# Fused attention and GELU kernel: batch 0's loads issued at once, weights in quarters, scores transposed by DMA

## The chip, the cores and the metric

The kernel runs on one core of one Trainium2 chip. Times are device microseconds of a whole execution; profiles give a span from the first to the last instruction, some 2 us shorter. PE is TensorE, PEld its weight loads, DVE is VectorE, ACT is ScalarE, POOL is GpSimd, and SP is the engine that issues most DMAs here.

## The reference

Four batches of cross-covariance attention (256 x 256 scores, summed over 6080 rows) feed a two-layer network with a tanh GELU.

```python
q, k, v = three arrays of (4, 6080, 256), float32          # tau = 1.0
qn = q / (norm(q, axis=1) + 1e-06);  kn = likewise k
s  = kn.transpose(0, 2, 1) @ qn / tau                      # (4, 256, 256)
a  = softmax(s, axis=-1)
x  = (v @ a).reshape(24320, 256)
y  = gelu_tanh(x @ w_in) @ w_out                           # w_in 256 x 2048, w_out 2048 x 256
```

## The kernel before

The product `a @ w_in` is formed first (`aw`), so each block of 512 rows needs only `hp = aw.T @ vT` (2048 x 512), the GELU on ACT into `g`, and `yp = g.T @ w_out`. Batch 0's q and k must be loaded, multiplied (`G`) and normalised before anything else can start. The same work for batches 1 to 3 is spread in small steps between the matmuls of the batch before: eight steps per block, twelve blocks per batch. Below, a slot is 128 rows, a chunk is the slots that one pair of loads (q and k) brings, and the column sums are the sums of squares from which the norms come. Of the loop over chunks (cut):

```python
first_chunks = chunks_of([12, 12, 5, 6, 4, 4, 2, 2], 2)   # slots of 128 rows of batch 0
fillers = [0, 0, 5, 7, 4, 3, 1, 0]                        # dummy matmuls meant to keep PE's clock up
...
for n, ch in enumerate(first_chunks):
    for to, sq, x in todo:
        nc.vector.tensor_copy(to, x)                       # fp32 -> bf16, DVE
        nc.scalar.activation(sq, x, AF.Square)             # ACT
    keep_clock(fillers[n])
    for s, rows in slots_of(ch, 128):
        gram(G, qkb, s, rows, ...)                         # 2 matmuls a slot
    pairs_of(n, sqb)          # pair sums on DVE, then column sums on PE (some chunks: sums only)
    ...                       # issue the loads of later chunks into the buffers now free
```

In the steps of a later batch (cut):

```python
for n in range(16):                       # the first 16 steps
    if n in (3, 9): load_qk(b, n // 6)    # loads of q and k of batch b, cast to bf16 by the DMA
    if b == 1 and n == 5: turn_v_on_pe(1) # block 1's v: 8 transposes on PE
    yield
...                                       # 54 steps: G and squares, then the norms
T = turned(Gs)                            # 4 fp32 transposes on PE
...
rsinv = row_sums(eT)
for fs in range(4):
    for ic in range(2):
        aw_part(eT, rsinv, aw_next, fs, ic); yield
```

From block 2 on, v is transposed by DMA two blocks ahead: `turn_v(nb + 2)` issues four DMA transposes of 128 x 256 on SP, `load_v(nb + 3)` loads v on POOL's queue.

## Time and profile before

The median of the runs was 754.13 us. These are the landmarks, from the timeline of the trace, in us from the start of the span:

| landmark | us |
|---|---|
| last piece of batch 0's q and k lands | 34.28 |
| last column sum of batch 0 starts on PE | 35.78 |
| first `hp` matmul starts | 40.06 |
| last `hp` matmul starts | 740.28 |
| end of the span | 751.98 |

I use two intervals of it as measures: **the start of the first `hp`**, which tells what the loading part costs, and **the time from the first to the last `hp`** (700.22 us), which tells what the stream costs. Both are read from one trace of each kernel.

### The profile page before, as it was taken

The page shows a single profiled execution, that of the slowest core. Times are in us where ns is not written, and L with a number is a line of the kernel's source. Part 1 is how long each engine was busy: PE and PEld are TensorE (multiplying, and loading weights), DVE is VectorE, ACT ScalarE, POOL GpSimd, SP SyncE. Part 2 cuts the span into 40 slices and gives each one's busy share as a digit, 9 for nine tenths or more (in the row PEclk, how much of TensorE's full clock was granted, in tenths as well). Part 3 has the DMA queues.
Part 4 walks back from the last instruction along what each step waited for, and adds up shares of the span by engine and source line. Part 5 has one row for each costly group of instructions (what it writes and reads, how often), then busy time and mean ns, then how long its engine had stood idle before and what let it go on. Part 6 is the DMA issues. An engine that isn't in the chain of part 4 may idle for free.

```text
span 752.0 us, 12341 instructions
## 1 busy us (share of the span) xinstructions
PE 726.4 (97%) x5186; PEld 502.3 (67%) x5274; DVE 284.3 (38%) x497; ACT 420.3 (56%) x411; POOL 80.8 (11%) x154
## 2 busy tenths in 40 slices
PE   2899999999999999999999999999999999999998
PEld 1656766776666766776666666776666666666666
DVE  3733556463501646554521265555351011011011
ACT  4875555556456555555555555555645655555552
POOL 1061111101012102101001102010101000000000
PEclk9999999999999999999999999999999999999999
DMA  9989685613237685824325876671413533322111
GB/s 369 400 205 200 104 150 139 132 43 69 70 72 144 114 163 108 164 63 75 71 57 117 141 119 124 150 143 46 69 43 85 105 85 70 69 75 54 41 57 57
DMA packets 80183, 85.69 MB, mean 114 GB/s; under 512 B 55424, under 2 KB 59136, under 8 KB 79616
## 3 DMA queue, kind: packets, MB, share of 16 engines
q0 software_dynamic: 14480, 30.87, 25.7%
q1 hardware_dynamic: 65344, 52.39, 24.4%
q10 hardware_dynamic: 304, 1.64, 0.5%
q8 instruction: 41, 0.67, 0.4%
q14 instruction: 14, 0.11, 0.0%
HBM read 78.91 MB, written 24.90 MB: 138 GB/s over the span
## 4 chain that ended last, share of the span: by engine, by line
PE 94%; DMA 3%; ACT 1%; issue 1%; DVE 0%; POOL 0%; SPq 0%; DVEq 0%; POOLq 0%
PE yp L528 44%; PE hp L602 43%; PE G L158 4%; PE ps L218 2%; ACT sq L269 1%; DMA st<-in_q_dram 1%; DMA st<-in_k_dram 1%; PE T L196 0%; POOL wout_bf L359 0%; PE yp L633 0%; PE cols L170 0%; DVE qk L267 0%; DVE aw L413 0%; DVE Gs L188 0%; ACT eT L383 0%
## 5 line engine op out<-in xcount | busy, mean ns | idle before, releaser
L606 ACT ACTIVATE g<-hp 128x1024 bf16<-128x1024 f32 (+1 forms) x384 | 389.8, 1015 | 307.0 <-PE hp L602 295.2
L528 PE MATMUL yp<-wout_bf,g 128*128 128x256 bf16 x3024 | 392.0, 273 | 1.6 <-POOL wout_bf L359 0.7
L602 PE MATMUL hp<-vT,aw 128*128 128x512 bf16 (+1 forms) x1456 | 383.9, 377 | 3.8 <-DVE aw L413 0.2
L528 PEld LDWEIGHTS <-g 128*128 128x128 bf16 x3024 | 295.9, 98 | 114.3 <-issue 1.2
L602 PEld LDWEIGHTS <-aw 128*128 128x128 bf16 x1536 | 149.9, 98 | 104.1 <-DVE aw L413 0.5
L545 DVE COPY ysb<-yp 128x512 f32<-128x512 f32 (+1 forms) x95 | 64.9, 683 | 396.5 <-PE yp L528 396.5
L460 DVE TENSOR_TENSOR acc<-acc,sq 128x512 f32<-128x512 f32 x141 | 97.6, 692 | 4.8
L459 DVE TENSOR_TENSOR sq<-qkb 128x512 bf16<-128x512 bf16 x141 | 58.9, 418 | 0.0
L158 PE MATMUL G<-qkb 128*128 128x256 bf16 x288 | 55.0, 273 | 0.0
L307 POOL DMA_DIRECT2D vb<-in_v_dram x47 | 25.9, 552 | 88.6 <-DMA vT<-vb 81.3
L227 DVE TENSOR_SCALAR aw<-ps,rsinv 128x512 bf16<-128x512 f32 x30 | 22.4, 749 | 23.5 <-PE ps L218 18.3
L158 PEld LDWEIGHTS <-qkb 128*128 128x128 bf16 x288 | 28.2, 98 | 3.3
L332 POOL CAST gate<-g 1x1 f32<-1x1 bf16 x24 | 5.9, 245 | 227.8 <-ACT g L606 227.8
L158 PE MATMUL G<-qk 128*128 128x256 bf16 x96 | 13.5, 298 | 15.8 <-DVE qk L267 15.8
L269 ACT ACTIVATE sq<-st 128x3072 bf16<-128x3072 f32 (+2 forms) x9 | 21.1, 2379 | 11.1 <-DMA st<-in_q_dram 8.2
L158 PEld LDWEIGHTS <-qk 128*128 128x128 bf16 x96 | 9.8, 106 | 19.1 <-DVE qk L267 16.6
L267 DVE CAST qk<-st 128x3072 bf16<-128x3072 f32 (+2 forms) x10 | 14.2, 1438 | 13.1 <-DMA st<-in_q_dram 10.0
L218 PE MATMUL ps<-win_bf,eT 128*128 128x512 bf16 x54 | 16.4, 379 | 0.2
L479 POOL TENSOR_TENSOR r<-r,half 128x4 f32<-128x4 f32 x3 | 3.1, 1042 | 103.4 <-DVE r L478 103.4
L82 POOL DMA_DIRECT2D qkb<-in_q_dram x24 | 12.9, 537 | 5.8 <-issue 4.3
L585 POOL COPY g<-gr 128x1024 bf16<-128x1024 bf16 x2 | 2.1, 1036 | 101.3 <-PE yp L528 101.3
L82 POOL DMA_DIRECT2D qkb<-in_k_dram x24 | 12.9, 539 | 0.0
(73 smaller groups left out, 109.0 us busy)
## 6 DMA issues: line engine op xcount, KB each, us to landing
out_dram<-ysb SPq DMA_DIRECT2D x44, 512.0 KB, 3.0
vb<-in_v_dram POOLq DMA_DIRECT2D x43, 256.0 KB, 6.2
qkb<-in_q_dram POOLq DMA_DIRECT2D x21, 384.0 KB, 4.6
qkb<-in_k_dram POOLq DMA_DIRECT2D x21, 384.0 KB, 6.4
st<-in_q_dram SPq DMA_DIRECT2D x2, 1536.0 KB, 11.8
vT<-vb SPq DMA_TRANSPOSE x184, 3.0
wst<-in_moe_w_in_dram SPq DMA_DIRECT2D x4, 512.0 KB, 7.5
wst<-in_moe_w_out_dram SPq DMA_DIRECT2D x2, 1024.0 KB, 11.7
```

Source lines behind the costliest of these rows:

```text
L82: engines[x].dma_start(out=dst[x][:, 0:size, :], in_=src[b, s0 * 128 : (s0 + size) * 128, :].rearrange("(p s) c -> p s c", s=size))
L158: nc.tensor.matmul(G[:, ic, :], lhsT=qk[1][:rows, s, ic * 128 : ic * 128 + 128], rhs=qk[0][:rows, s, :], start=first and ic == 0, stop=las ...
L218: nc.tensor.matmul(ps, lhsT=eT[:, jc, ic * 128 : ic * 128 + 128], rhs=win_bf[:, jc, fs * 512 : fs * 512 + 512], start=jc == 0, stop=jc == 1)
L227: nc.vector.tensor_scalar_mul(dst, ps, scale)
L269: nc.scalar.activation(sq, x, AF.Square)
L307: nc.gpsimd.dma_start(out=t[:, 0:n, :], in_=v_rows[r0 : r0 + n * 128, :].rearrange("(p s) c -> p s c", s=n))
L459: nc.vector.tensor_mul(sq[:rows], flat, flat)
L460: nc.vector.tensor_add(acc[:rows], acc[:rows], sq[:rows])
L528: nc.tensor.matmul(yp[:rows, at, :], lhsT=g[:, fc, s * 128 : s * 128 + rows], rhs=wout_bf[:, fc, :], start=fc == 0, stop=fc == FC - 1)
L545: nc.vector.tensor_copy(ysb[:, s0 : s + 1, :], yp[:, 0 : s + 1 - s0, :])
L602: nc.tensor.matmul(hp[:, j, :cols], lhsT=aw[:, cc, fc * 128 : fc * 128 + 128], rhs=vT[:, cc, :cols], start=cc == 0, stop=cc == 1)
L606: nc.scalar.activation(g[:, 2 * i : 2 * i + 2, :cols], hp[:, :, :cols], AF.Gelu_apprx_tanh)
```

## The change

Its intent: (1) batch 0's loads get homes of their own (the still unused tiles of `g`, `aw` and the staging pool), so that no load waits for a buffer; (2) the weights come in quarters, with output-weight rows contiguous per partition, for which the columns of `aw` are sorted; (3) the scores of batches 1 to 3 leave PE: their fp32 bits are split into upper and lower halves, turned by DMA and put together again, and the row sums come two steps later; (4) the chain to the first `hp` is cut finer. The core of the diff, with cuts marked:

```diff
-    first_chunks = chunks_of([12, 12, 5, 6, 4, 4, 2, 2], 2)
-    fillers = [0, 0, 5, 7, 4, 3, 1, 0]
+    first_chunks = chunks_of([2, 12, 12, 5, 4, 4, 4, 2, 1, 1], 3)
+    fillers = [0, 0, 0, 5, 6, 5, 4, 2, 1, 0]
+    CASTS_POOL = (6, 7)
...
+    g_homes = [gp.tile([128, FC, 512], BF16, tag="g", name="g").bitcast(FP32) for _ in range(2)]
+    aw_homes = [...]; st_homes = [...]
+    for n, ch in enumerate(first_chunks):
+        load_chunk((nc.sync, nc.scalar if n < 1 else nc.sync), staged[n][0], 0, ch, 2)
...
-        for x in ((2, 3) if n == 0 else (4, 5) if n == 1 else (n + 4,)):
-            stage_chunk(x)
...
+    for fs in range(4):
+        w, T = w_quarter(), t_of(fs)
+        rows_of_w = moe_w_out[fs * 512 : fs * 512 + 512, :]
+        nc.sync.dma_start(out=w.rearrange("p (e t c) -> p e t c", t=T, c=256),
+                          in_=rows_of_w.rearrange("(e p t) c -> p e t c", p=128, t=T))
+        nc.gpsimd.tensor_copy(wout_bf[:, fs * 4 : fs * 4 + 4, :], w.rearrange(...))
...
-        T = turned(Gs)
+        bits = Gs.bitcast(U16).rearrange("p a (j h) -> p h a j", h=2)
+        for h in range(2):
+            nc.vector.tensor_copy(apart[:, h], bits[:, h])
+            for ic in range(2):
+                nc.sync.dma_start_transpose(
+                    out=crossed[:, h, :, ic * 128 : ic * 128 + 128], in_=apart[:, h, ic, :])
+        for _ in range(6):
+            yield
+        bits = T.bitcast(U16).rearrange("p a (i h) -> p h a i", h=2)
+        for h in range(2):
+            nc.vector.tensor_copy(bits[:, h], crossed[:, h])
```

More of the change, by code (lines that the diff above doesn't have):

```diff
@@ L10 @@
 BF16 = mybir.dt.bfloat16
+U16 = mybir.dt.uint16
 AF = mybir.ActivationFunctionType
@@ L93 @@
     n_all = S_ALL + 1
-    first_chunks = chunks_of([12, 12, 5, 6, 4, 4, 2, 2], 2)
-    TAIL, SHARED = 4, 6
-    fillers = [0, 0, 5, 7, 4, 3, 1, 0]
-    staged = []
+    first_chunks = chunks_of([2, 12, 12, 5, 4, 4, 4, 2, 1, 1], 3)
+    n_chunks = len(first_chunks)
+    TAIL = 4
+    fillers = [0, 0, 0, 5, 6, 5, 4, 2, 1, 0]
+    SQUARES_DVE = (6, 7)
+    CASTS_POOL = (6, 7)
     def halves(pool, tag, dtype, size, most=SMAX):
@@ L107, in halves, with slot_pair @@
         return [t.rearrange("p a b c -> p (a b) c") for t in tiles], None
-    def stage_chunk(n):
-        if n < len(first_chunks):
-            _, size, rem = first_chunks[n]
-            if n < SHARED:
-                st, whole = halves(stage, "st", FP32, size)
-            else:
-                _, size, rem = first_chunks[n - 2]
-                whole = staged[n - 2][1][:, :, size + rem :, :]
-                st = [whole[:, x] for x in range(2)]
-                rem = False
-            if rem:
-                nc.gpsimd.memset(whole[:, :, size, :], 0.0)
-            load_chunk((nc.sync, nc.scalar if n < 1 else nc.sync), st, 0, first_chunks[n], 2)
-            staged.append((st, whole))
-    for n in range(2):
-        stage_chunk(n)
+    def slot_pair(whole, lo, hi):
+        return [whole[:, x, lo:hi, :] for x in range(2)], whole[:, :, lo:hi, :]
+    g_homes = [gp.tile([128, FC, 512], BF16, tag="g", name="g").bitcast(FP32) for _ in range(2)]
+    aw_homes = [awp.tile([128, 2, D], BF16, tag="aw", name="aw").bitcast(FP32).rearrange(
+        "p x (s c) -> p x s c", c=256) for _ in range(2)]
+    st_homes = [stage.tile([128, 2, SMAX, 256], FP32, tag="st", name="st") for _ in range(4)]
+    shared = st_homes[3]
+    staged = [
+        slot_pair(shared, 0, 2),
+        ([g[:, 0:12, :] for g in g_homes], None),
+        ([t.rearrange("p a b c -> p (a b) c") for t in st_homes[:2]], None),
+        slot_pair(st_homes[2], 0, 6),
+        slot_pair(aw_homes[0], 0, 4),
+        slot_pair(aw_homes[1], 0, 4),
+        ([g[:, 12:16, :] for g in g_homes], None),
+        slot_pair(shared, 2, 4),
+        slot_pair(shared, 4, 5),
+        slot_pair(shared, 5, 6),
+    ]
+    nc.gpsimd.memset(staged[3][1][:, :, 5, :], 0.0)
+    for n, ch in enumerate(first_chunks):
+        load_chunk((nc.sync, nc.scalar if n < 1 else nc.sync), staged[n][0], 0, ch, 2)
     ident = const.tile([128, 128], FP32)
@@ L147, with t_of, sorted_columns, pieces @@
     win_v = moe_w_in.rearrange("(c p) d -> p c d", p=128)
-    wout_v = moe_w_out.rearrange("(t p) d -> p t d", p=128)
+    def t_of(fs):
+        return 2 if fs == 0 else 4
+    def sorted_columns(ps, fs):
+        return ps.rearrange("a (e p t) -> a e t p", p=128, t=t_of(fs))
+    def pieces(dst, fs):
+        return dst.rearrange("a (e t p) -> a e t p", p=128, t=t_of(fs))
     def keep_clock(n, pool=pH, tag="h"):
@@ L190, in scaled, with row_sums @@
         return Gs
-    def turned(Gs):
-        T = pA.tile([128, 2, 256], FP32, tag="a", name="T")
-        for ic in range(2):
-            for jc in range(2):
-                nc.tensor.matmul(T[:, jc, ic * 128 : ic * 128 + 128],
-                                 lhsT=Gs[:, ic, jc * 128 : jc * 128 + 128],
-                                 rhs=ident, is_transpose=True)
-        return T
-    def row_sums(eT):
-        rs = pA.tile([128, 512], FP32, tag="a", name="rs")
+    def row_sums(eT, rs=None):
+        if rs is None:
+            rs = pA.tile([128, 512], FP32, tag="a", name="rs")
         for ic in range(2):
@@ L212, in row_sums, with aw_part @@
         return rsinv
-    def aw_part(eT, rsinv, aw, fs, ic, ps=None, act=False):
+    def aw_part(eT, rsinv, aw, fs, ic, ps=None):
         if ps is None:
@@ L222, in aw_part @@
                 start=jc == 0, stop=jc == 1)
-        dst, scale = aw[:, ic, fs * 512 : fs * 512 + 512], rsinv[:, ic : ic + 1]
-        if act:
-            nc.scalar.activation(dst, ps, AF.Copy, scale=scale)
-        else:
-            nc.vector.tensor_scalar_mul(dst, ps, scale)
+        dst = pieces(aw[:, ic, fs * 512 : fs * 512 + 512], fs)
+        nc.vector.tensor_scalar_mul(dst, sorted_columns(ps, fs), rsinv[:, ic : ic + 1])
     G = pA.tile([128, 2, 256], FP32, tag="a", name="G")
     cols = pA.tile([128, 512], FP32, tag="a", name="cols")
-    n_chunks = len(first_chunks)
     seen, summed = 0, 0
@@ L265 @@
             todo = [[y[:, :, 0:hi] for y in (qk_whole, sq_whole, whole)]]
+        if n in CASTS_POOL:
+            nc.gpsimd.tensor_copy(qkb[1][:, 0:hi], st[1])
+            todo = [(qkb[0][:, 0:hi], None, st[0])]
         for to, sq, x in todo:
-            nc.vector.tensor_copy(to, x)
-            if n != n_chunks - 2:
-                nc.scalar.activation(sq, x, AF.Square)
-        if n == n_chunks - 2:
-            nc.scalar.activation(sqb[1][:, 0:hi], st[1][:, 0:hi], AF.Square)
+            nc.vector.tensor_copy(to[:, 0:hi] if whole is None else to, x)
+            if sq is not None and n not in SQUARES_DVE:
+                nc.scalar.activation(sq[:, 0:hi] if whole is None else sq, x, AF.Square)
+        if n in SQUARES_DVE:
+            nc.scalar.activation(sqb[1][:, 0:hi], st[1], AF.Square)
             nc.vector.tensor_mul(sqb[0][:, 0:hi], qkb[0][:, 0:hi], qkb[0][:, 0:hi])
@@ L279 @@
             waiting = None
-        if n < 2:
+        if n < 3:
             pairs_of(n, sqb)
@@ L343, in load_qk, with w_quarter @@
             loaded_of[b, n] = views, t
-    def flat_stage(n):
-        w = stage.tile([128, 2, SMAX, 256], FP32, tag="st", name="wst")
-        return w.rearrange("p a b c -> p (a b c)")[:, 0:2048].rearrange("p (c d) -> p c d", c=n)
-    for half in range(2):
-        w = flat_stage(2)
-        for x in range(2):
-            c0 = half * 1024 + x * 512
-            nc.sync.dma_start(out=w[:, :, x * 512 : x * 512 + 512], in_=win_v[:, :, c0 : c0 + 512])
-            nc.gpsimd.tensor_copy(win_bf[:, :, c0 : c0 + 512], w[:, :, x * 512 : x * 512 + 512])
-        load_v(1 + half)
-    for half in range(2):
-        w = flat_stage(8)
-        nc.sync.dma_start(out=w, in_=wout_v[:, half * 8 : half * 8 + 8, :])
-        nc.gpsimd.tensor_copy(wout_bf[:, half * 8 : half * 8 + 8, :], w)
+    w_homes = []
+    def w_quarter():
+        n = len(w_homes)
+        if n % 3 == 0:
+            t = stage.tile([128, 2, SMAX, 256], FP32, tag="st", name="wst")
+            t = t.rearrange("p a b c -> p (a b c)")
+        else:
+            t = w_homes[-1]
+        w_homes.append(t)
+        return t[:, n % 3 * 1024 : n % 3 * 1024 + 1024]
+    for fs in range(4):
+        w = w_quarter().rearrange("p (c d) -> p c d", c=2)
+        step = 256 if fs == 0 else 512
+        for lo in range(0, 512, step):
+            c0 = fs * 512 + lo
+            nc.sync.dma_start(out=w[:, :, lo : lo + step], in_=win_v[:, :, c0 : c0 + step])
+            nc.gpsimd.tensor_copy(win_bf[:, :, c0 : c0 + step], w[:, :, lo : lo + step])
+        if fs % 2:
+            load_v(1 + fs // 2)
+    for fs in range(4):
[3 more added lines that the diff above has]
+                          in_=rows_of_w.rearrange("(e p t) c -> p e t c", p=128, t=T))
+        nc.gpsimd.tensor_copy(wout_bf[:, fs * 4 : fs * 4 + 4, :], w.rearrange("p (f c) -> p f c", c=256))
     r = smx.tile([128, 4], FP32, tag="r", name="r")
@@ L366, with turn_v0 @@
     Gs = scaled(G, r)
-    vps = []
-    for cc in range(2):
-        p = pH.tile([128, 2, 512], FP32, tag="h", name="vps")[:, 0, :]
+    vps = pH.tile([128, 2, 512], FP32, tag="h", name="vps")
+    spare = pH.tile([128, 2, 512], FP32, tag="h", name="spare")
+    def turn_v0(cc):
         for s in range(4):
-            nc.tensor.matmul(p[:, s * 128 : s * 128 + 128],
+            nc.tensor.matmul(vps[:, cc, s * 128 : s * 128 + 128],
                              lhsT=v0[:, s, cc * 128 : cc * 128 + 128],
                              rhs=ident, is_transpose=True)
-        vps.append(p)
-    keep_clock(1, pY, "y")
-    T = turned(Gs)
-    keep_clock(1, pY, "y")
+    turn_v0(0)
+    T = [pY.tile([128, 512], FP32, tag="y", name="T") for _ in range(2)]
+    for ic in range(2):
+        for jc in range(2):
+            nc.tensor.matmul(T[jc][:, ic * 128 : ic * 128 + 128],
+                             lhsT=Gs[:, ic, jc * 128 : jc * 128 + 128],
+                             rhs=ident, is_transpose=True)
+    turn_v0(1)
     vT0 = vts.tile([128, 2, 512], BF16, tag="vT", name="vT")
-    nc.vector.tensor_copy(vT0[:, 0, :], vps[0])
+    nc.vector.tensor_copy(vT0[:, 0, :], vps[:, 0, :])
     eT = smx.tile([128, 2, 256], BF16, tag="eT", name="eT")
@@ L382, with first_aw @@
     for jc in range(2):
-        nc.scalar.activation(eT[:, jc, :], T[:, jc, :], AF.Exp, scale=r[:, jc : jc + 1])
-    nc.scalar.activation(vT0[:, 1, :], vps[1], AF.Copy)
+        nc.scalar.activation(eT[:, jc, :], T[jc][:, 0:256], AF.Exp, scale=r[:, jc : jc + 1])
+    nc.scalar.activation(vT0[:, 1, :], vps[:, 1, :], AF.Copy)
     firsts = []
-    def first_aw(n, jc, pool=pY, tag="y"):
+    def first_aw(n, jc, pool=pA, tag="a"):
         if jc == 0:
@@ L400 @@
     first_aw(1, 0)
-    rsinv = row_sums(eT)
+    rsinv = row_sums(eT, spare[:, 0, :])
     first_aw(0, 1)
@@ L404 @@
     for n in (2, 3):
-        first_aw(n, 0, pA, "a")
+        first_aw(n, 0, pY, "y")
         first_aw(n, 1)
-    for n in range(4):
+    for n, t, act in ((0, 0, False), (1, 0, True), (0, 1, True), (1, 1, False), (2, None, False), (3, None, False)):
         ic, lo = n % 2, n // 2 * 256
-        dst, scale = aw[:, ic, lo : lo + 256], rsinv[:, ic : ic + 1]
-        if n == 1:
-            nc.scalar.activation(dst, firsts[n][:, 0:256], AF.Copy, scale=scale)
+        dst = aw[:, ic, lo : lo + 256].rearrange("a (t p) -> a t p", t=2)
+        ps = firsts[n][:, 0:256].rearrange("a (p t) -> a t p", t=2)
+        if t is not None:
+            dst, ps = dst[:, t], ps[:, t]
+        scale = rsinv[:, ic : ic + 1]
+        if act:
+            nc.scalar.activation(dst, ps, AF.Copy, scale=scale)
         else:
-            nc.vector.tensor_scalar_mul(dst, firsts[n][:, 0:256], scale)
+            nc.vector.tensor_scalar_mul(dst, ps, scale)
     nc.scalar.activation(dummy, ones_f, AF.Gelu_apprx_tanh)
-    aw_left = [(fs, ic, *((pA, "a") if fs == 2 else (pY, "y"))) for fs in range(1, 4) for ic in range(2)]
+    aw_left = [(fs, ic, *((pY, "y") if fs == 2 else (pA, "a"))) for fs in range(1, 4) for ic in range(2)]
     def more_aw(n):
@@ L486, in attention_steps @@
         Gs = scaled(G, r)
+        apart = split.tile([128, 2, 2, 256], U16, tag="apart", name="apart")
+        crossed = split.tile([128, 2, 2, 256], U16, tag="crossed", name="crossed")
+        T = split.tile([128, 2, 256], FP32, tag="T", name="T")
+        bits = Gs.bitcast(U16).rearrange("p a (j h) -> p h a j", h=2)
+        for h in range(2):
+            nc.vector.tensor_copy(apart[:, h], bits[:, h])
+            for ic in range(2):
+                nc.sync.dma_start_transpose(
[5 more added lines that the diff above has]
+            nc.vector.tensor_copy(bits[:, h], crossed[:, h])
         yield
-        yield
-        T = turned(Gs)
         eT = smx.tile([128, 2, 256], BF16, tag="eT", name="eT")
@@ L495, in attention_steps @@
         else:
-            th = smx.tile([128, 2, 256], FP32, tag="th", name="th")
-            den = smx.tile([128, 2, 256], FP32, tag="den", name="den")
+            th = split.tile([128, 2, 256], FP32, tag="th", name="th")
+            den = split.tile([128, 2, 256], FP32, tag="den", name="den")
             for jc in range(2):
@@ L507, in attention_steps @@
                     op0=ALU.add, op1=ALU.mult)
+            yield
+            yield
             yield
```

## The prediction

Passages that no trace of this case shows are cut from it (and from two expectations below), and the cuts are marked. The sum has all its terms, -1.3 - 0.7 - 0.3 + 0 = -2.3 us. In the hand count of the loading part the terms are cut: 23 dummies, 44 `G` matmuls at 0.109 us and 80 column sums at 0.025 us came to 11.7 us with a figure for a dummy that the trace doesn't show; at the 0.216 us between two dummies in the trace they come to 11.8.

> **What bounds the kernel now.** I read the page first (totals, slices, chain), then a table of stretches, then what the TensorE (PE) waited for, then the timeline of the first 52 us and of one place in mid-run. From the page:
>
> ```profile
> PE 726.4 (97%) x5186; PEld 502.3 (67%) x5274; DVE 284.3 (38%) x497; ACT 420.3 (56%) x411; POOL 80.8 (11%) x154
> ...
> L528 PE MATMUL yp<-wout_bf,g 128*128 128x256 bf16 x3024 | 392.0, 273 | 1.6 <-POOL wout_bf L359 0.7
> L602 PE MATMUL hp<-vT,aw 128*128 128x512 bf16 (+1 forms) x1456 | 383.9, 377 | 3.8 <-DVE aw L413 0.2
> ```
>
> PE has hardly any idle time, and its two large groups wait 5.4 us in all. The list of PE's waits is as short:
>
> ```profile
> PE G L158 <- DVE qk L267: 15.8, 3, 14.4
> PE yp L528 <- POOL wout_bf L359: 0.7, 1, 0.7
> ```
>
> So only the first 40 us and one wait of 0.7 us are open to better scheduling. The table of stretches (columns: length, busy time of PE, weight loads, DVE, ACT, POOL, granted clock, DMA share, GB/s) says what the first 40 us are:
>
> ```profile
> 10.00:20.00 10.00, 5.08 (x48) 3.82 (x48) 7.95 (x6) 9.10 (x4) 1.07 (x1) 1.00 1.00 420
> 20.00:35.00 15.00, 14.06 (x176) 10.65 (x178) 11.68 (x14) 12.11 (x7) 0.00 (x0) 1.00 1.03 402
> 35.00:40.00 5.00, 4.10 (x46) 2.90 (x44) 2.57 (x9) 3.91 (x9) 2.70 (x3) 1.00 1.04 340
> ```
>
> From 10 to 35 us the DMA engines are full (share 1.00 and more) at 402 to 420 GB/s while batch 0's q and k come in. After that a short serial chain (roots, scaling, transposes, exponential, first products) leads to the first `hp` matmul at 40.06 us, and from there PE runs to 748 us practically without a hole. Is PE at its true rate there? The timeline at 182 us answers (start, length, then the instructions merged):
>
> ```profile
> 182.42 1.04 PE L528 MATMUL yp<-wout_bf,g 128*128 128x256 bf16 x8
> 182.62 1.02 ACT L606 ACTIVATE g<-hp 128x1024 bf16<-128x1024 f32 x1 [0.71 <-PE hp L602]
> 183.19 0.47 PEld L196 LDWEIGHTS T<-ident,Gs 128*128 128x128 f32 x4
> 183.30 0.60 PE L196 MATMUL T<-ident,Gs 128*128 128x128 f32 x4
> ```
>
> Eight `yp` matmuls in 1.04 us, the last one 0.273 long, start (1.04 - 0.273) / 7 = 0.11 us apart; likewise the four fp32 transposes `T`, (0.60 - 0.273) / 3 = 0.109. They stand flush between their neighbours. Each matmul taken out of this stream is worth its spacing, not its 0.273 us.
>
> [...]Here a DMA transpose takes 3.0 us from issue to landing (median)[...].
>
> **The change part by part.**
>
> *Scores turned by DMA (batches 1 to 3).* Removed from PE: 4 transposes x 3 batches x 0.109 = **1.3 us**, all on the path. Added: per batch 4 DMA transposes, and 4 DVE copies of 128x512 16-bit elements with a step of two, which I put at the 0.69 us of this page's 128x512 DVE rows[...]: 3 x 4 x 0.69 = 8 us of DVE, idle for 62% of the span. The copies back come six steps later. A step (4 `hp` at 0.216 and 8 `yp` at 0.109) is 1.74 us, so the transposes have about 10 us: issue takes 1.3 us each on SP, landing 3. That fits. Count of steps: 81 before the last products, now 88, plus 8, is 96, exactly the 12 blocks x 8 steps of a batch. The last products fall in the last steps, but those hold the columns that the next batch uses last, six steps on. No wait follows.
>
> *Row sums two steps later.* Before, neither they nor the products after them made PE wait in mid-run (they aren't in the list of waits). **0 us.**
>
> *Weights in quarters, output weights in contiguous rows.* The timeline at 50 us shows the one wait there is:
>
> ```profile
> 49.88 1.90 POOL L359 CAST wout_bf<-wst 128x2048 bf16<-128x2048 f32 x1 [2.02 <-PE hp L602]
> ...
> 51.83 0.60 PE L528 MATMUL yp<-wout_bf,g 128*128 128x256 bf16 x4 [0.71 <-POOL wout_bf L359]
> ```
>
> The second 1 MB half of the output weights landed at 49.8 us and took a 1.9 us cast. [...]casts of about 1.0 us per quarter, bring the third quarter (needed at 51 us) in by about 48 us by my estimate. Gain **0.7 us**. The permuted columns cost only strides in DVE's reads of PSUM; I count 0.
>
> *Chain before the first product.* Each half of the transposed scores has its own bank, dummy matmuls fall away, the first `aw` pieces are 128 columns (half the work before `hp` may start), two of them on ACT. In the old trace the exponential waited for T until 38.08 us; with the first half of T done one transpose earlier (0.16 us) and the `aw` piece before `hp` shorter by about 0.2 us, I take **0.3 us**.
>
> *Batch 0 loads at once.* I expect least of what the title promises. The old loads ran first in, first out at 1.00 share already: the last one was issued at 25.61 us and took 8.7 us to land (34.3 us), waiting behind others. 12.45 MB at the measured 400 to 420 GB/s take some 30 us[...]. The new order has the same bytes, so the last piece lands at about 34 us again. Two opposite effects follow. For: the last chunk is one slot, not two, so less is left after it, and no chunk waits for a buffer: up to -0.8 us. Against: in program order there are 23 dummy matmuls (were 20)[...], that PE must pass. Running the order of the new kernel by hand with the old durations (cast of 3072 elements 1.75, square 2.75, G matmul 0.109, column sum 0.025), chunk 2's k half lands at 19.6, is cast by 21.3, its squares end at 22.3, its pair sums at 23.3, and PE gets to the dummies before chunk 3 at 24.7. What is left from there is[...] 11.7 us, end 36.4; the old kernel ended this part at 35.9. So +0.5 to +1 us if the dummies are passed late, -0.8 if PE really has holes there. Middle: **0**.
>
> Sum: -1.3 - 0.7 - 0.3 + 0 = -2.3 us; I round it to -2.1, since some of the gain in the chain may be lost to ACT, which must also copy half of `vT0` there. 754.1 - 2.1 = **752.0**.
>
> **Rivals.** (1) *The loads really gain*: DMA had holes that share hides, and the first `hp` starts 2 us earlier. For it: the share of the first 10 us is only 0.82; and between 26.9 and 29.0 us a 0.5 MB piece took 2.1 us where its neighbours took 1.3. Against: the queue was never empty then. Time: 750. (2) *A new steady wait*: DVE's copies or SP's blocked queue delay `ysb` copies or `vT` transposes, or the last steps of a batch now hold PE back. For: all 96 steps are used, no slack. Against: `yp` has two buffers of four steps (7 us) each, `vT` is fetched two blocks ahead. Time: 754 to 756. (3) *The dummies bind*: PE passes the loading part 1 us late and eats half the gain. Time: 753.
>
> **Range and chances.** 752.0, range 750.2 to 753.8: (1) is the lower end, (3) with some of (2) the upper. Runs spread by 0.4 us. A 2% change is 15 us; more than the whole compressible part could give, and a loss of 15 us would need a wait in every block. Faster 0.01, same 0.98, slower 0.01.
>
> **What would show it.** Right: the first `hp` at 39.5 to 40.5 us; no `yp` wait on POOL; no fp32 `T` on PE after 40 us; PE flush between 60 and 740 us; last q/k piece landing at 33.5 to 34.5 us. Wrong: landing well before 33 us or the first `hp` before 39 (rival 1), PE waits on `aw` or for `yp`'s banks at batch boundaries (rival 2), or a wait on `vT`.

## The result, and the profile after

The changed kernel took 753.89 us in the median (753.38 to 754.40, four runs), the kernel before 754.01 in the same rounds; the ratio is 0.9999, 95% interval 0.9981 to 1.0016. The predicted 752.0 us was too low, and the measured time lies just above the range.

The totals and the two large groups, from the page of the changed kernel:

```profile
PE 727.2 (97%) x5181; PEld 502.5 (67%) x5271; DVE 289.9 (39%) x513; ACT 419.6 (56%) x414; POOL 82.3 (11%) x159
...
L572 PE MATMUL yp<-wout_bf,g 128*128 128x256 bf16 x3024 | 392.0, 273 | 1.0
L646 PE MATMUL hp<-vT,aw 128*128 128x512 bf16 (+1 forms) x1453 | 383.3, 377 | 3.8 <-ACT aw L440 0.2
```

The wait of `yp` on POOL is gone. PE's whole list of waits shows no new large one: those of `G` are 1.1 us shorter in all (15.8 before), that of `T` is 0.5 us longer (0.4 before), and that of `ps` (0.4 before) is gone. Waits alone don't tell why the first `hp` came later:

```profile
PE G L177 <- DVE qk L277: 14.7, 3, 7.2
PE T L399 <- DVE Gs L207: 0.9, 1, 0.9
PE hp L646 <- ACT aw L440: 0.2, 1, 0.2
```

The table of stretches shows where the difference is (the columns are those of the prediction's table; the one to look at is the third from the end, the granted clock):

```profile
10.00:20.00 10.00, 5.07 (x48) 3.82 (x48) 6.22 (x5) 7.12 (x4) 0.00 (x0) 1.00 1.00 423
20.00:35.00 15.00, 14.04 (x152) 10.30 (x154) 11.10 (x14) 10.68 (x7) 1.65 (x2) 0.89 1.04 393
35.00:40.00 5.00, 4.09 (x57) 3.10 (x54) 1.46 (x5) 2.67 (x6) 2.53 (x4) 1.00 1.02 348
```

The DMA is as full as before (1.04 at 393 GB/s), and PE as busy (14.04 against 14.06 us), but between 20 and 35 us PE did it at a mean granted clock of 0.89 and with 152 matmuls in place of 176. PE's timeline from 17 us, first of the kernel before, then of the changed one, names the place:

```profile
18.73 0.74 PE L170 MATMUL cols<-ones_bf,pair 128*128 128x1 bf16 x24
20.70 2.79 PE L158 MATMUL G<-qk 128*128 128x256 bf16 x24 [1.24 <-DVE qk L267]
23.33 0.74 PE L170 MATMUL cols<-ones_bf,pair 128*128 128x1 bf16 x24
```

```profile
17.82 0.74 PE L189 MATMUL cols<-ones_bf,pair 128*128 128x1 bf16 x24
20.89 4.22 PE L177 MATMUL G<-qk 128*128 128x256 bf16 x24 [2.32 <-DVE qk L277]
24.94 0.74 PE L189 MATMUL cols<-ones_bf,pair 128*128 128x1 bf16 x24
```

The same 24 `G` matmuls took 2.79 us before and 4.22 us after. They follow a gap in which PE waits for the second 12-slot chunk: 1.2 us before, 2.3 us after. The trace's record of the granted clock says full from 17.01 until 20.43 us, half until 23.84, then full until the last microsecond: one stretch of 3.41 us at half clock. (Before 17.01 the record has no entry and the table above counts 1.00; the `G` matmuls start 0.213 us apart until then and 0.109 after, so 17.01 is where the clock first rose; in the trace of the kernel before it is 17.93.) The kernel before has no such stretch before the first `hp` in its trace. In some of its executions it may have one: of 11 that ran beside the first experiments, four had a mean clock of 0.997 or 0.998 and took 754.55 to 754.98 us, the seven at 1.000 took 753.51 to 754.51. All four executions of the changed kernel had 0.995 to 0.998.

The landmarks, before and after:

| landmark | before | after | difference |
|---|---|---|---|
| last q, k piece lands | 34.28 | 34.56 | +0.28 |
| last column sum starts | 35.78 | 37.30 | +1.52 |
| first `hp` | 40.06 | 41.47 | +1.41 |
| from the first to the last `hp` | 700.22 | 698.13 | -2.09 |
| from the last `hp` to the end | 11.70 | 12.01 | +0.31 |
| span | 751.98 | 751.61 | -0.37 |

So the stream gained 2.09 us, close to the 2.0 us that I had put down for it, and the loading part gave 1.41 back. (The end of the span takes 11.7 to 11.8 or 12.0 us in all the kernels below; I did not look into it.)

Two more lines. The scores' turn on DVE, from the groups after 60 us:

```profile
L530 DVE COPY T<-crossed 128x512 uint16<-128x512 uint16 x6 | 2.7, 453 | 2.1 <-DMA crossed<-apart 2.1
L522 DVE COPY apart<-Gs 128x512 uint16<-128x512 uint16 x6 | 2.3, 423 | 0.1
```

The 12 copies took 5.0 us and PE waited for none of them. And "at once" is not at once; SP's issues in the changed kernel (start, length):

```profile
7.96 0.33 SPq L83 DMA_DIRECT2D aw<-in_q_dram  x1
11.67 0.33 SPq L83 DMA_DIRECT2D aw<-in_k_dram  x1
15.36 0.33 SPq L83 DMA_DIRECT2D aw<-in_q_dram  x1
```

The program has no buffer to wait for here, but each of these issues comes 0.02 us after an earlier load has landed (7.94, 11.65, 15.34 us): batch 0's loads use eight semaphores in turn (101 to 103 and 106 to 110 in the trace), and the tenth SP load uses that of the load issued at 1.18 us (103) again and waits for it. The last one is issued at 27.72 us (25.61 before). With the DMA engines as full as before (1.04 against 1.03 from 20 to 35 us), I take it that this cost nothing, but no run issued the loads really at once. It says that the part of the change that names it did not happen as written.

### The profile page after: what moved, and what is told of

Read it like the earlier page. It is cut to its first block, busy times and chain, and to the rows that moved or that the text cites. A ratio compares the mean times of both kernels' runs of the same rounds, so it can differ in the third digit from the quotient of the medians.

```text
span 751.6 us, 12382 instructions
## 1 busy us (share of the span) xinstructions
PE 727.2 (97%) x5181; PEld 502.5 (67%) x5271; DVE 289.9 (39%) x513; ACT 419.6 (56%) x414; POOL 82.3 (11%) x159
## 4 chain that ended last, share of the span: by engine, by line
PE 96%; DMA 2%; issue 1%; DVE 1%; SPq 0%; ACT 0%; DVEq 0%
PE yp L572 44%; PE hp L646 43%; PE G L177 5%; DMA st<-in_k_dram 2%; PE ps L229 2%; PE idle L173 1%; PE cols L189 0%; PE yp L677 0%; DVE qk L277 0%; SPq L83 0%; PE T L399 0%; DVE vT L404 0%; DVE Gs L207 0%; ACT aw L440 0%; PE vps L391 0%
## 5 line engine op out<-in xcount | busy, mean ns | idle before, releaser
L589 DVE COPY ysb<-yp 128x512 f32<-128x512 f32 (+1 forms) x95 | 64.9, 683 | 393.9 <-PE yp L572 393.9
L235 DVE TENSOR_SCALAR aw<-ps,rsinv 128x512 bf16<-128x512 f32 x30 | 22.4, 749 | 22.2 <-PE ps L229 15.8
L177 PE MATMUL G<-qk 128*128 128x256 bf16 x96 | 15.6, 324 | 14.7 <-DVE qk L277 14.7
L279 ACT ACTIVATE sq<-st 128x3072 bf16<-128x3072 f32 (+2 forms) x6 | 10.6, 1768 | 5.8 <-DMA st<-in_k_dram 2.6
L664 POOL COPY gr<-g 128x1024 bf16<-128x1024 bf16 x2 | 2.1, 1035 | 79.9 <-ACT g L650 79.9
```

Source lines behind the costliest of these rows:

```text
L177: nc.tensor.matmul(G[:, ic, :], lhsT=qk[1][:rows, s, ic * 128 : ic * 128 + 128], rhs=qk[0][:rows, s, :], start=first and ic == 0, stop=las ...
L235: nc.vector.tensor_scalar_mul(dst, sorted_columns(ps, fs), rsinv[:, ic : ic + 1])
L279: nc.scalar.activation(sq[:, 0:hi] if whole is None else sq, x, AF.Square)
L589: nc.vector.tensor_copy(ysb[:, s0 : s + 1, :], yp[:, 0 : s + 1 - s0, :])
```

## The experiments

(The expectations call the stretch at half clock the cold window.) Theory A: the fall of the clock, and the dummies that PE must pass afterwards, hold the first `hp` back. Rival B: the landings bind. Rival C: fewer dummies only bring the clock down elsewhere. A fourth theory, D, came from the first four runs. Times are medians; the ratio is against the kernel before in the same rounds.

### Bridging the gap

```diff
-    fillers = [0, 0, 0, 5, 6, 5, 4, 2, 1, 0]
+    fillers = [0, 0, 10, 5, 6, 5, 4, 2, 1, 0]
```

> The changed kernel with 10 dummy matmuls put before chunk 2's products (none there now), the other 23 kept. Theory A, cold window plus dummies: TensorE idles from 18.6 to 20.9 us, the clock falls to half[...] (20.4 to 23.8 us), and chunk 2's 24 products take 3.95 us in place of 2.8. With the gap bridged they take 2.6 to 2.9 us, the first hp starts at 40.2 to 40.6 us (now 41.5), time 752.7 us. Rival B, the landings bind (last k piece at 34.6 us): the first hp stays at 41.5 us, time 753.9 us. If the fall of the clock does not come from the gap, it will show again and nothing changes.

Measured: the clock held, the 24 matmuls took 2.78 us, the last column sum started at 36.03 and the first `hp` at 40.07 us (41.47 without). PE's timeline there (one of the ten dummies is missing from the trace):

```profile
19.12 2.10 PE L173 MATMUL idle<-filler 128*128 128x512 bf16 x9
21.06 2.78 PE L177 MATMUL G<-qk 128*128 128x256 bf16 x24
```

B falls: the last piece landed at 34.39 us, as ever. But the time was 754.85 us (753.11 to 756.76), ratio 1.0017, interval 1.0003 to 1.0030: no gain at all, and a far larger spread. The list of PE's waits of its profile has a line that neither kernel had:

```profile
PE hp L646 <- DMA vT<-vb: 1.0, 1, 1.0
```

### No dummies, and fewer

```diff
+    fillers = [0, 0, 0, 0, 0, 0, 0, 0, 0, 0]        # e2
+    fillers = [0, 0, 10, 1, 2, 3, 3, 2, 1, 0]       # e3
```

> The changed kernel with no dummy matmul in the loading part at all (23 removed). Theory A: TensorE catches up after the cold window, waits for data again, and the first hp starts 4.0 us after the last column sum, which can't be before about 35.5 us: first hp at 39.2 to 39.8 us, time 751.8 us. Rival C[...]: without dummies the clock falls to half in the later part too, products at 0.2 us, first hp at 40.5 us or later, and the steady part may start cold: 753.5 us or more. Rival B, landings bind: 41.5 us, 753.9 us.

> The changed kernel with the 10 bridging dummies and 12 in place of 23 after them. Theory A: both losses gone, no cold window, no queue on TensorE at the last chunk; first hp at 39.0 to 39.6 us, time 751.3 us. Rival B: 41.5 us and 753.9 us. Rival C: as the no-dummy run if 12 are too few.

Measured: with none, the clock fell twice (22.3 to 25.7 and 32.5 to 35.9 us) and the first `hp` came at 40.68 us, so C has its share: taking all dummies out gains less than bridging. The first of the two stretches at half clock followed a shorter gap than the changed kernel's:

```profile
21.04 4.15 PE L177 MATMUL G<-qk 128*128 128x256 bf16 x24 [1.51 <-DVE qk L277]
```

The time was 754.43 us (751.60 to 755.89), ratio 1.0001. With the gap bridged and 12 dummies the clock held, the first `hp` came at 40.29 us, no earlier than with all 23, and the time was 753.21 us (752.45 to 754.96), ratio 0.9990, interval 0.9978 to 1.0002. Both profiles have `hp` waiting for `vT`, 1.9 and 1.6 us. The expected 751 to 752 us did not come.

### The old loading part in the changed kernel

The chunks, staging, dummies and loop of batch 0 taken from the kernel before, all else changed (the edit is that part of the diff above, reversed).

> The changed kernel with the old loading part of batch 0 (old chunks, homes, dummies), all else as changed. Theory A: the loading part is what cost the gain. First hp at 39.7 to 40.1 us, the part from the first to the last hp as in the changed kernel (698.1 us, old 700.2), time 751.9 us. Rival: the rest of the change costs as well, e.g. the new chain with two transposes of v0 around the scores or the quarter casts; then the first hp stays above 40.5 us and the time near 753 us.

Measured: first `hp` at 40.02 us, no fall of the clock, as expected. Time 753.51 us (752.69 to 757.79), ratio 1.0002, not 751.9. From the first to the last `hp` it took 699.12 us, not 698.1, and 0.8 us of that is again a wait on `vT`. Four kernels with an early first `hp`, four times the same wait. That makes theory D.

### Theory D: a new wait

In the bridged kernel's timeline on PE, the last columns of block 1 are followed by block 2's first `hp`:

```profile
63.42 0.82 PE L572 MATMUL yp<-wout_bf,g 128*128 128x256 bf16 x6
65.20 1.02 PE L646 MATMUL hp<-vT,aw 128*128 128x512 bf16 x4 [0.96 <-DMA vT<-vb]
```

Block 2 is the first whose v is turned by DMA, about 24 us after the first `hp`. Its four transposes, issue to landing in us, and the first loads of batch 1's q and k:

| kernel | fourth transpose issued | landed | block 2's `hp` starts | first q load issued |
|---|---|---|---|---|
| before | 52.81 | 61.54 | 64.84 | 52.95 |
| changed | 53.68 | 65.03 | 65.48 | 52.17 |
| changed, bridged | 54.52 | 65.06 | 65.20 (late) | 51.12 |

In the kernel before POOL was busy with the second large weight cast until 51.8 us, and issued the loads of v, q and k after it; with quarters, POOL is free earlier, those loads come up to 1.8 us earlier, and in these traces the fourth transpose, issued 0.9 to 1.7 us later, lands 3.5 us later. The theory is that it is held up by those loads. In the changed kernel the first of the four transposes, issued at 49.76 us, took 2.4 us to land, the fourth, among those loads, 11.4; `vT` was there with 0.45 us to spare, only because the first `hp` was late.

Two ways of taking the cause away. Block 2's v turned on PE:

```diff
+            if b == 1 and n == 13:
+                turn_v_on_pe(2)
...
-            turn_v(nb + 2)
+            if nb > 0:
+                turn_v(nb + 2)
```

> The changed kernel with the 10 bridging dummies, and block 2's v turned by 8 bf16 transposes on TensorE (as block 1's already is) in place of 4 DMA transposes. Theory D, a new wait: once the first hp starts at 40.1 us, block 2's vT, turned by DMA beside the loads of q, k and v, lands only at about 65 us and hp waits for it, 1.0 us in the trace of the bridged kernel and up to some 4 us in other executions. With that transpose off the DMA: no wait on vT, from the first to the last hp 698.1 + 8 x 0.055 = 698.6 us (bridged run: 699.25), time 752.5 us, and all runs within 1 us (bridged: 753.1 to 756.8). Rival E, the spread comes from something else, such as the clock: spread and mean as in the bridged run, 754.8 us.

The loads of q and k issued later (loads of v share POOL's queue, and one of them moves too, from 56.9 to 64.9 us):

```diff
-            if n in (3, 9):
-                load_qk(b, n // 6)
+            if n in (10, 14):
+                load_qk(b, n // 14)
```

> The changed kernel with the 10 bridging dummies, and the two first loads of the next batch's q and k issued at steps 10 and 14 in place of 3 and 9. Theory D: with less traffic beside them, block 2's DMA transposes land by about 62 us, no wait on vT; from the first to the last hp 698.1 us, time 752.2 us, spread under 1 us. Rival E: nothing changes (754.8 us, spread over 3 us). If the transposes are slow for another reason than these loads, the wait on vT stays at about 1 us.

Measured: both have no wait on `vT`. With PE's transposes 698.58 us from the first to the last `hp` (698.6 expected), 752.85 us (752.33 to 752.97), ratio 0.9977; with late loads 698.13 us, 752.35 us (752.05 to 752.67), ratio 0.9972, interval 0.9960 to 0.9985. (In the first one's trace the clock rose only at 19.68 us, PE reached the second 12-slot chunk at 21.72 in place of 21.06 us, and the first `hp` came at 40.73 us, so its time is not the best of that kernel.) The spread was 0.64 and 0.62 us, that of the bridged kernel 3.65 us. With late loads the fourth transpose landed at 57.73 us, and the same place on PE reads:

```profile
63.44 0.82 PE L572 MATMUL yp<-wout_bf,g 128*128 128x256 bf16 x6
64.09 1.03 PE L646 MATMUL hp<-vT,aw 128*128 128x512 bf16 x4
```

D is shown for the traces: two different ways of taking the wait away both end it. That the loads hold up the transposes shows in all traces: in the six with late loads the fourth transpose landed at 57.73 to 58.88 us, in the nine others that turn this block by DMA at 61.54 to 66.62 us. The time of the first load alone doesn't set it: five traces issue it at 52.14 to 52.25 us, and there the transpose landed at 62.22, 62.46, 65.03, 65.89 and 66.62 us. That D also explains the spread is not shown: the bridged kernel was timed on another chip than these two and was not run again beside them. The clock, rival E's example, doesn't explain it either: one of the bridged kernel's two executions of 756.76 us had a mean clock of 1.000.

### Old loading part with late loads

> The changed kernel with the old loading part of batch 0 and the late loads of q and k. Theory D: the first hp at 40.0 us, no wait on vT, 698.1 us from the first to the last hp: time 752.1 us, as with the new loading part bridged, i.e. the new loading part in itself is worth nothing. Rival: it is worth something hidden by the clock; then this is slower than the bridged kernel with late loads by 0.5 us or more.

Measured: first `hp` at 40.03 us, 698.13 us to the last one, 751.69 us (751.53 to 752.79), ratio 0.9967, interval 0.9954 to 0.9979. The new loading part with its 23 dummies, even with the clock kept, is worth nothing against the old one.

### The kernels themselves again, and late loads in each

> The changed kernel as it is, once more, for a second trace and more times. Theory: the cold window during chunk 2's products is there again or the first hp is earlier and hp waits for block 2's vT in its place; either way the time is near 754 us, since what the first loses less the second takes.

> The kernel before with only the late loads of q and k (steps 10 and 14). Theory D: the old kernel's block 2 vT landed (61.5 us) before it was needed (63.7), so there is little to win: from the first to the last hp 700.2 us, time 753.9 us, ratio 0.999 to 1.0. Rival: late loads are a gain in themselves, 752.5 us; then the gains of the earlier runs aren't the new wait's.

> The changed kernel with only the late loads of q and k, no bridging dummies. If the cold window is what holds it: the clock falls again, first hp at 41.4 to 41.8 us, no wait on vT to remove, time 753.7 us, as the changed kernel. If the wait on vT was what cost most in the untraced executions of the changed kernel: 753.0 us or less with a smaller spread.

Measured: the changed kernel again had its clock at half from 21.64 to 25.05 us, first `hp` at 41.78 us, no wait on `vT` (the fourth transpose landed at 62.22 us), and took 753.77 us (752.93 to 754.51), ratio 0.9992. The kernel before with late loads took 754.26 us, ratio 0.9996, interval 0.9982 to 1.0010: late loads in themselves are no gain. Its trace has the first `hp` at 40.92 us, behind loads that landed at 35.14 us (34.28 in the trace of the kernel before), and 700.09 us from the first to the last `hp`. So with one and the same loading part the first `hp` differs by 0.9 us between two traces, and single landmarks are no surer than that.

The changed kernel with late loads only took 753.49 us (752.04 to 754.68). Its profiled run, by luck, kept its clock:

```profile
18.75 0.81 PE L189 MATMUL cols<-ones_bf,pair 128*128 128x1 bf16 x24
21.03 2.79 PE L177 MATMUL G<-qk 128*128 128x256 bf16 x24 [1.47 <-DVE qk L277]
```

There the clock rose only at 19.25 us, the sums before ended later, and the gap was 1.5 us. This run, with a mean clock of 1.000, took 752.04 us; the other five, at 0.995 to 0.998, took 753.45 to 754.68. One stretch of 3.41 us at half clock is 3.41 x 0.5 / 752 = 0.0023 of the mean, which is how 0.998 and less can be read. On that reading, an estimate, the price of such a stretch within one kernel is 1.4 us or more. The traces agree: with one such stretch the first `hp` of this loading part came at 41.47, 41.67 and 41.78 us, with none at 40.06 here and, bridged with the same 23 dummies, at 40.07, 40.09 and 40.73. My expectation for it was right in the time and did not foresee the lucky run.

### What the two gains of the stream are worth

The scores turned on PE again, at the same steps (the kernel's old four transposes in place of copies and DMA), and the old weight loads and casts without sorted columns; one look each (a single execution, its state unknown).

> The changed kernel with the scores of batches 1 to 3 turned on TensorE again, at the same steps. One look. From the first to the last hp: 698.1 + 12 x 0.109 = 699.4 us if the DMA turn is worth its issue slots and nothing else; 698.1 if those slots were free.

> The changed kernel with the old loads and casts of the weights (halves of 1 MB, rows of 1 KB, no sorted columns). One look. From the first to the last hp: 698.1 + 0.7 = 698.8 us if the quarters took away just the old wait of yp on the cast; 698.1 if that wait was moved by something else. Theory D also says that the old cast, which keeps POOL busy until about 52 us, issues the next loads of q and k later (first at 52.5 us or after, 51.1 in the bridged kernel).

Measured: with the scores on PE, 699.45 us from the first to the last `hp`, 1.32 more than 698.13; expected 1.3. (Its one execution had its clock at half from 20.1 to 26.9 us, so its time, 756.27 us, is not compared.) With the old weights, 698.07 us and no wait of `yp` on POOL: my expectation of 698.8 missed. With the first `hp` at 41.67 us the second half of the output weights is ready in time. So in the changed kernel the quarters save nothing; the late start does. The first load of q was issued at 53.35 us there, and the fourth transpose landed at 61.54 us, as theory D had it.

### Both causes removed, and the quarters where they count

```diff
+    fillers = [0, 0, 10, 5, 6, 5, 0, 0, 0, 0]       # with late loads; e14 also with the old weights
```

> The changed kernel with the 10 bridging dummies, the late loads of q and k, and no dummy before the last four chunks (7 of 23 taken out). If these dummies bind once the clock is kept, the last column sum comes up to 0.5 us earlier than 36.05 us and the first hp at 39.6 us, time 751.9 us; if the landings and the casts bind, first hp at 40.0 to 40.1 us, time 752.3 us.

> The kernel with bridging dummies, late loads and seven dummies fewer (751.4 us), with the old loads and casts of the weights. If the quarters are worth the old wait once the first hp is early (39.4 us): a wait of yp on the cast of 0.7 us or more is back, from the first to the last hp 698.8 to 699.8 us, time 752.1 to 753.1 us. If not: 698.1 us and 751.4 us.

Measured: without the last seven dummies the last column sum starts at 35.37 us (36.05 with them) and the first `hp` at 39.41 us (40.09). Time 751.41 us (751.30 to 752.77), ratio 0.9963, interval 0.9951 to 0.9976: the fastest kernel, 0.37% ahead of the one before. With the old weights in it:

```profile
PE yp L562 <- POOL wout_bf L368: 1.2, 2, 0.7
```

699.55 us from the first to the last `hp` and 752.85 us. Where the first `hp` is early, the quarters are worth 1.4 us.

## Why the prediction was wrong

**The step that failed** is the one on batch 0's loads: "Middle: **0**". It took about the mean of -0.8 and +1, and the measured figure was +1.52 us at the last column sum. The hand count behind it assumed 0.109 us for every `G` matmul; in the changed kernel 14 of the second 12-slot chunk's 24 ran 0.213 us apart, at half clock. Its other part held: 11.7 us from the dummies before chunk 3 to the end, against 11.75 in the bridged kernel (24.28 to 36.03 us). The bridged kernel, the same program but for the ten dummies that keep the clock, starts its last column sum at 36.03 us, so the stretch at half clock cost 37.30 - 36.03 = 1.27 us, and 0.25 us is what else the new order costs. I had read the dummies in the code as work that PE must pass and not asked what the idle gap without dummies, which grew from 1.2 to 2.3 us, would do to the clock. It grew because the new order lets PE start on the first 12-slot chunk 0.89 us earlier (13.49 against 14.38) while the second is ready 0.19 us later, and because in this trace the clock also rose 0.92 us earlier.

In the five traces with a stretch at half clock before the first `hp`, PE had waited for the second 12-slot chunk for 1.51 us (no dummies), 1.83 (the changed kernel again), 2.3 (old weights), 2.32 (the changed kernel) and 2.59 us (scores on PE). In the kernel before it waited 1.24 us and in the lucky run 1.47, and the clock stayed full; with ten dummies in the gap of the same kernel it stayed full too. So during that chunk the clock fell only where the gap was left open. How long a gap must be for it, and what else decides it, these single traces don't show.

The rest of the miss is small. Against the sum of -2.3 us the span fell by 0.37: +1.52 from the loading part in place of 0, 0.19 lost in the chain, 0.31 at the end of the span, which the prediction did not count, and 0.09 more gained in the stream. "Runs spread by 0.4 us" rested on three runs; the 11 later ones of the kernel before spread by 1.5 us, so the times alone hardly resolve a gain of 2 us.

**Rival 3, the dummies bind,** was right in its direction (PE passes the loading part late), but not in its cause: the dummies are the smaller part, and that its 753 us lies nearer to the measured time than 752.0 is luck. The last seven cost 0.68 us (36.05 - 35.37), measured only once the clock is kept.

**The last landing** was right: 34.56 us for "about 34 us again". The prediction's ground was the bytes at 400 to 420 GB/s, and from 20 to 35 us they came at 393 (402 before); its "first in, first out" is in the trace of the kernel before, where batch 0's 18 loads landed in the order of their issue, from 10.88 to 34.28 us. That the loads would still be issued one after another, up to 27.72 us, was not foreseen.

**The chain before the first product:** 4.28 us before (35.78 to 40.06), 4.17 after: 0.1 us in place of 0.3. In ten other traces with the same new chain it took 4.03 to 4.05 us, a gain of 0.23 to 0.25, so the prediction was nearer than this one trace says. Its 0.2 us for the shorter `aw` piece was my estimate: pieces of 128 columns took 0.35 to 0.37 us in the changed kernel, pieces of 256 took 0.48 before.

**The scores turned by DMA:** 1.3 us predicted, 1.32 measured, and no wait at the batch boundaries though all 96 steps are used. DVE paid 5.0 us, not 8, and the transposes took 2.3 us from issue to landing, not 3.

**The quarters:** "Gain **0.7 us**" was the size of the wait, and the wait is gone, but in this kernel the later start alone removes it (698.07 us with the old weights). The cast of the third quarter ended at 48.55 us, "about 48" by the prediction's estimate; that the size of the pieces helps was not shown. The sorted columns cost nothing that shows: DVE's `aw` copies of 128 x 512 took 0.749 us on average before and after. Row sums two steps later: no wait before or after; I did not test them alone.

**Rival 2, a new steady wait,** named "a wait on `vT`" among the things to look for, and set it aside because "`vT` is fetched two blocks ahead". It did not occur in the two traces of the changed kernel, but it stands right behind: as soon as the loading part is repaired, it takes the gain. My argument counted blocks and not the traffic on the DMA engines at 50 to 64 us. That its 754 us fits the measured time is luck. How long this wait is in executions that were not traced is not shown.

**What stays open:** why the spread of the bridged kernel reaches 3.65 us although its one trace shows a wait of 1.0 us (other traces of an early first `hp` show up to 1.9), why the transposes land up to 4.4 us apart behind loads issued at the same time, and what makes the end of the span 11.7 or 12.0 us long.

## What to carry to other kernels

Removing a wait pays only down to the next one: read from the trace when each later input arrives and how much it has to spare, for a start that comes earlier moves every deadline forward, and loads that are freed earlier can crowd others (here up to 1.8 us earlier, and a transpose landed 3.5 us later). Before closing or opening a gap on TensorE in a loading phase, look at the granted clock there, since a gap of 2.3 us here cost another 1.3 us after it had ended. And a gain of 2 us in a stream of 700 is visible in the trace, as an interval between two instructions, long before it is visible in the times.
